# mLSTM attention and two mixture-of-experts layers on one core: full-row tiles for the decay spread and the third logit block, gate work and constants moved into the units

## The chip, the cores and the metric

The kernel runs on one core of one Trainium2 chip. The metric is the time of one execution on the device in microseconds (us), lower is better. Several executions are timed and the median is taken; one more is recorded by the hardware profiler.

## The reference

Three layers follow each other. Attention is a gated linear recurrence over 768 steps for 2 batches and 8 heads of 40 columns; its output, 1536 tokens of 320 columns, goes through a layer that gives each token to one of 8 experts (192 tokens each, best logits first), and then through a dense layer of 4 experts weighted by given probabilities.

```python
for t in range(S):                                   # attention
    m_new = np.maximum(f_gate[:, :, t] + m, i_gate[:, :, t])
    f_stab = np.exp(f_gate[:, :, t] + m - m_new)
    i_stab = np.exp(i_gate[:, :, t] - m_new)
    m = m_new
    C = f_stab * C + i_stab * outer(v_t, k_t)
    n = f_stab * n + i_stab * k_t
    y[:, :, t] = sigmoid(o_t) * (C @ q_t) / np.maximum(np.abs(n @ q_t), 1.0)
logits = x @ w_gate                                  # first expert layer
order = np.argsort(-logits.flatten())                # tokens are given out in this order
out[mask_e] = np.maximum(x[mask_e] @ w1[e], 0) @ w2[e]
p = domain_probs / (domain_probs.sum(-1) + 1e-9)     # second expert layer
out += p[:, e:e + 1] * (np.maximum(x @ w1[e], 0.0) @ w2[e])
```

## The kernel before

All work is issued in the order of the program; each engine takes its own instructions strictly in that order, and semaphores tie the engines together. The change lies wholly in `attention()`, which fills the first 120 us or so; routing, the first expert layer and the second follow.

Attention cuts the 768 steps into 6 chunks of 128 steps. A **unit** is one chunk of one batch with its 8 heads; the 12 units run in the order (0,0), (0,1), (1,0), ... and are numbered n = 0 to 11. For each unit:

- `spread_d` (L244, L246) builds in PSUM (tile `db`, 2 buffers) the sums of the log decay gates over pairs of steps: one matmul with the identity adds a causal mask (`maskb`), and a second one spreads a row of the decay over all 128 partitions. That row is kept as a high and a low part (`dhi`, `dlo`) in `drow`, so this second matmul has 2 rows: `one2` of [2, 128] against `drow` of [2, 512]. The rows get into `drow` by small DMAs (L218), issued by SyncE (SP), one for each chunk and part.
- `exps` (L300, L303) takes the exponential on ScalarE (tile `gg`); `scores` (L287) multiplies keys and queries into `st` (2 buffers); `weigh` (L309) multiplies the two on VectorE into `pm`, which also frees the `st` buffer; `products` (L336, L342, L346) multiplies with the values, with the carried state `C`, and makes the update of the state.
- `epilogue` works on VectorE: `tq` (L371) or a copy (L375), the sum, the normaliser, `xr` (L402), and the update of `C` (L385) in between. It then sends `xr` to DRAM (L404), for which SP also waits for a small load of `dprob` (L401).
- `logit` and `logit2` are the three transposes (L416), the copy to `xt` (L420, L421) and the product with the gate weights `wg` (L433) for earlier units. The 320 columns go in blocks of 128, 128 and 64. The logits are read by VectorE (L435), and the PSUM buffer of a transpose is free again only after that.

`weave` takes matmuls in turn from the generators of a step: in the step of unit n stand the scores of unit n+1, the products of unit n, the spread of unit n+2 and the logits of units n-3 and n-2. The epilogue of unit n follows the step. Matmuls on zeros (`warm`, L254) are put in places where TensorE would wait at the start; `CR['W']` and `CR['W1']` are their numbers there.

`gate(c0, c1)` (L206 to L221) computes the gates of chunks c0 to c1 for all 16 heads on VectorE: two scans and six or seven elementwise instructions, with the DMAs to `drow` between them; `gate_t` transposes the result on TensorE (L233) and copies it to `gtr` (L236). Gates are computed as `gate(0, 1)`, `gate(1, 2)` and, before the loop over the units, `gate(2, NCH)`.

`routing_consts()` (L90 to L123) fills the tables for the routing, 20 instructions on VectorE and the rest on GpSimd, in one block after the epilogue of unit 2. At the top of every second step, `load(c + 2)` and `load_kv(c + 2)` (L154, L161) issue the queries, keys and values of a later chunk on SP, 1320 KB and 648 KB.

## Time and profile before

| | |
|---|---|
| median of 3 executions | 663.55 us (663.23 to 669.81) |
| profiled execution, its own time | 666.88 us |
| span of its trace | 665.2 us |
| granted TensorE clock, mean over the span | 0.975 |
| TensorE matmul busy | 635.1 us (95%) |
| VectorE, ScalarE, GpSimd busy | 281.3, 172.9, 112.8 us |

Times inside the trace count from the start of the span. PE is TensorE, PEld its weight loads, DVE is VectorE, ACT ScalarE, POOL GpSimd, SP SyncE; SPq is SP's sequencer, which issues DMAs. The granted clock is 1 where TensorE runs at 2.4 GHz and 0.5 where it runs at 1.2 GHz.

### The profile page before, as it was taken

Reading aid. Unit: us, or ns where it says so; the run is one execution under the profiler, and the core shown is the slowest. Engines: PE = TensorE matmul, PEld = TensorE weight load, DVE = VectorE, ACT = ScalarE, POOL = GpSimd, SP = SyncE. Lnnn points to the kernel's source line nnn. Section 1 sums busy time; section 2 is a strip of 40 time slices with the busy share of each in tenths; the row PEclk is TensorE's granted clock in tenths of the full one; section 3 lists DMA queues with packets and bytes.
Section 4 is the critical chain, followed back from the end, with each engine's and each line's share of the span. In section 5 each row is a group of like instructions: output and inputs, shape, how many; then the busy total and the mean of one; then the engine's idle time right before and its main releaser. Section 6 shows DMA issues by size and latency. Waiting matters only on the chain.

```text
span 665.2 us, 10604 instructions
## 1 busy us (share of the span) xinstructions
PE 635.1 (95%) x4255; PEld 545.8 (82%) x4265; DVE 281.3 (42%) x1011; ACT 172.9 (26%) x432; POOL 112.8 (17%) x142
## 2 busy tenths in 40 slices
PE   6989999989899999799999999999999999999996
PEld 3778788658588878688898988989889898998986
DVE  4864657774766775531131313313132231322231
ACT  4444331002132323453231112321123211111120
POOL 2321300120122011220331003320023300002022
PEclk7986999899999999999999999999999999999999
DMA  8666421540555233760221001210000000001011
GB/s 218 200 172 161 120 75 31 186 174 3 179 174 179 89 126 140 294 233 0 65 64 48 0 1 33 90 53 1 1 1 0 1 1 0 1 1 41 0 40 39
DMA packets 13503, 53.78 MB, mean 81 GB/s; under 512 B 3639, under 2 KB 5607, under 8 KB 10679
## 3 DMA queue, kind: packets, MB, share of 16 engines
q1 hardware_dynamic: 9695, 27.76, 14.5%
q0 software_dynamic: 3584, 25.26, 10.5%
q8 instruction: 33, 0.54, 0.3%
q10 hardware_dynamic: 176, 0.09, 0.1%
q14 instruction: 15, 0.12, 0.1%
HBM read 49.05 MB, written 3.96 MB: 80 GB/s over the span
## 4 chain that ended last, share of the span: by engine, by line
PE 65%; issue 20%; DVE 10%; POOL 2%; DMA 1%; ACT 1%; POOLq 0%; DVEq 0%; ACTq 0%
PE y L579 5%; PE y L577 5%; PE y L578 5%; PE y L993 5%; PE z L1007 5%; PE z L563 4%; PE z L565 4%; PE z L564 4%; PE st L287 4%; PE z L1087 3%; PE acc L336 3%; PE z L568 2%; PE z L569 2%; POOL out_dram L589 2%; PE z L1000 2%
## 5 line engine op out<-in xcount | busy, mean ns | idle before, releaser
L1227 DVE SCALAR_TENSOR_TENSOR h2l<-z,h2h 128x512 fp32r<-128x512 f32 x96 | 66.4, 692 | 246.1 <-ACT h2h L1226 244.9
L1226 ACT ACTIVATE h2h<-z 128x512 fp32r<-128x512 f32 x96 | 57.3, 597 | 258.7 <-PE z L569 254.4
L579 PE MATMUL y<-wh,h2l 128*128 128x320 f32 x384 | 118.7, 309 | 0.0
L577 PE MATMUL y<-wh,h2h 128*128 128x320 f32 x384 | 118.4, 308 | 0.0
L578 PE MATMUL y<-wl,h2h 128*128 128x320 f32 x384 | 118.1, 308 | 0.0
L563 PE MATMUL z<-X2h,wh 128*128 128x512 f32 x192 | 76.7, 399 | 0.6 <-ACT yt L1027 0.6
L577 PEld LDWEIGHTS y<-wh,h2h 128*128 128x128 f32 x384 | 72.1, 188 | 4.4
L565 PE MATMUL z<-X2h,wl 128*128 128x512 f32 x192 | 75.7, 394 | 0.0
L564 PE MATMUL z<-X2l,wh 128*128 128x512 f32 x192 | 75.3, 392 | 0.0
L578 PEld LDWEIGHTS y<-wl,h2h 128*128 128x128 f32 x384 | 72.1, 188 | 3.8
L579 PEld LDWEIGHTS y<-wh,h2l 128*128 128x128 f32 x384 | 72.0, 188 | 0.0
L552 POOL TENSOR_TENSOR wl<-raw,wh 128x512 fp32r<-128x512 f32 x27 | 34.9, 1292 | 182.6 <-ACT wh L547 182.6
L993 PE MATMUL y<-h,w 128*128 128x192 f32 x256 | 56.0, 337 | 0.2 <-ACT h L1010 0.2
L1007 PE MATMUL z<-xt,w 128*128 128x192 f32 x256 | 54.5, 335 | 0.0
L993 PEld LDWEIGHTS y<-h,w 128*128 128x128 f32 x256 | 41.6, 190 | 2.8 <-issue 1.3
L287 PE MATMUL st<-qk 120*128 120x128 f32 x192 | 43.3, 319 | 0.5 <-issue 0.3
L565 PEld LDWEIGHTS z<-X2h,wl 128*128 128x128 f32 x192 | 36.0, 188 | 9.4
L1007 PEld LDWEIGHTS z<-xt,w 128*128 128x128 f32 x256 | 41.9, 190 | 2.2 <-issue 1.8
L563 PEld LDWEIGHTS z<-X2h,wh 128*128 128x128 f32 x192 | 36.0, 188 | 5.3 <-ACT yt L1027 0.9
L564 PEld LDWEIGHTS z<-X2l,wh 128*128 128x128 f32 x192 | 36.0, 188 | 4.6
L1087 PE MATMUL z<-hot,ones 128*128 128x396 bf16 x199 | 38.3, 330 | 0.4 <-DVE logits L435 0.3
L1010 ACT ACTIVATE h<-z 128x192 f32<-128x192 f32 x64 | 21.0, 330 | 66.8 <-PE z L1007 59.8
(242 smaller groups left out, 923.0 us busy)
## 6 DMA issues: line engine op xcount, KB each, us to landing
raw<-in_m2w_dram SPq DMA_DIRECT2D x20, 512.0 KB, 3.7
qk<-in_qk_dram SPq DMA_DIRECT2D x5, 1320.0 KB, 9.9
kv<-in_kv_dram SPq DMA_DIRECT2D x6, 648.0 KB, 10.5
x_dram<-xr SPq DMA_DIRECT2D x12, 162.0 KB, 2.0
sig<-in_og_dram SPq DMA_DIRECT2D x1, 1280.0 KB, 14.3
raw<-in_m2w_dram SPq DMA_DIRECT2D x4, 256.0 KB, 3.5
qk<-in_qk_dram SPq DMA_DIRECT2D x2, 480.0 KB, 6.4
sig<-in_og_dram SPq DMA_DIRECT2D x1, 640.0 KB, 5.3
```

What stands on the lines that cost most here:

```text
L287: T.matmul(p[:, i], QK[c][:, 6 + h], QK[c][:, 3 * b + (4 * u + i) // 3], start=True, stop=True)
L563: T.matmul(z, hi[:, c], xh[:, k], start=(k == 0), stop=False)
L564: T.matmul(z, hi[:, c], xl[:, k], start=False, stop=False)
L565: T.matmul(z, lo[:, c], xh[:, k], start=False, stop=False)
L577: T.matmul(y[:, :DM], hh[:, ts], hi[:, c], start=(f == 0), stop=False)
L578: T.matmul(y[:, :DM], hh[:, ts], lo[:, d], start=False, stop=False)
L579: T.matmul(y[:, :DM], hl[:, ts], hi[:, c], start=False, stop=(f == NF - 1))
L993: T.matmul(ys[0][:, i * CAP:(i + 1) * CAP], w[:, c:c + P], hs[f], start=(f == 0 and i == 0), stop=(f == NF - 1), skip_group_check=True)
L1007: T.matmul(at(f), w[:, c:c + P], xt[:, k], start=False, stop=(k == 1), skip_group_check=True)
L1087: T.matmul(z[:, :396], ones, hot, start=True, stop=True)
L1226: A.activation(hh, z, AF.Relu)
L1227: V.scalar_tensor_tensor(hl, z, 0.0, hh.bitcast(F32), op0=OP.max, op1=OP.subtract)
```

## The change

- `drow` becomes three tiles of [128, 16 heads, 128], taken in turn by chunk (c % 3), zero but for the two rows of the decay. `one2` becomes [128, 128], zero but for two rows of ones. The spread matmul so has 128 rows. Two of the tiles are cleared by ScalarE copies at the start, the third by a GpSimd memset before the loop.
- The third block of the logits takes columns 192 to 319 in place of 256 to 319; the third block of `wg` has zeros in the rows that stand for columns already counted. Transpose and product have 128 rows and columns, and one ScalarE copy fills `xt` in place of two.
- `gate()` returns a list of steps. Chunks 2 and 3 are put into the epilogue of unit 0 and chunks 4 and 5 into those of units 2 (five steps) and 3 (four steps), each behind the steps of the state update. `gate_t(1, 2)` moves to just before the loop, `gate_t(2, 4)` to the top of step 2, `gate_t(4, NCH)` to the top of step 5.
- `routing_consts()` issues its GpSimd part at once (in a slightly different order) after unit 2 and returns 13 small VectorE pieces, of which three are issued after each epilogue from unit 2 on.
- `CR['W']` goes from 9 to 15 and `CR['W1']` from 3 to 8.

```diff
     def routing_consts():
-        V.tensor_scalar(tri, jp, 0.0, None, op0=OP.is_gt)
...
+        return [lambda: V.tensor_scalar(tri, jp, 0.0, None, op0=OP.is_gt),
+                lambda: V.tensor_scalar(trin, jp, 0.0, -1.0, op0=OP.is_gt, op1=OP.mult),
+                lambda: V.tensor_scalar(triun, jp, 0.0, -1.0, op0=OP.is_lt, op1=OP.mult),
+                lambda: (V.memset(crow, 0.0), V.memset(crow[:1, 1:2], float(CAP)), V.memset(pen, 0.0)),
...
-            drow = big.tile([2, NCH, BH, P], F32, name="drow")
-            one2 = big.tile([2, P], F32R, name="one2")
+            drow = [big.tile([P, BH, P], F32, name=f"drow{i}") for i in range(3)]
+            one2 = big.tile([P, P], F32R, name="one2")
...
+            for i in range(2):
+                A.activation(drow[i].rearrange("p h t -> p (h t)").rearrange("p (i t) -> p i t", t=512).bitcast(F32R),
+                             wup[:, None].to_broadcast([P, 4, 512]), AF.Copy)
             load_o(0, CR['SO'])
             sigm(0, CR['SO'])
...
+                def send(i, d):
+                    for c in range(c0, c1):
+                        nc.sync.dma_start(drow[c % 3][i:i + 1], d[:, c * P:(c + 1) * P].bitcast(F32))
+
+                ops = [lambda: V.tensor_tensor_scan(mm[:, s1], ft[:, s], it[:, s], mm[:, c0 * P:c0 * P + 1],
+                                                    op0=OP.add, op1=OP.max),
+                       lambda: V.tensor_add(dl[:, s], ft[:, s], mm[:, s]),
+                       lambda: V.tensor_sub(dl[:, s], dl[:, s], mm[:, s1])]
                 if c0 == 0:
-                    V.memset(dl[:, 0:1], 0.0)
+                    ops.append(lambda: V.memset(dl[:, 0:1], 0.0))
+                ops += [lambda: V.tensor_tensor_scan(g3[64:64 + BH, s], rst[:, s], dl[:, s], 0.0, op0=OP.mult, op1=OP.add),
+                        lambda: V.tensor_sub(io[:, s], it[:, s], mm[:, s1]),
+                        lambda: (V.tensor_scalar(dhi[:, s], g3[64:64 + BH, s], 0.0, None, op0=OP.add), send(0, dhi)),
+                        lambda: (V.tensor_sub(dlo[:, s], g3[64:64 + BH, s], dhi[:, s].bitcast(F32)), send(1, dlo)),
...
-                    T.matmul(d, one2, drow[:, c, h:h + 4].bitcast(F32R), start=False, stop=True)
+                    T.matmul(d, one2, drow[c % 3][:, h:h + 4].bitcast(F32R), start=False, stop=True)
...
-            V.memset(one2.bitcast(F32), 1.0)
+            V.memset(one2.bitcast(F32), 0.0)
+            V.memset(one2[:2].bitcast(F32), 1.0)
...
-            gate(1, 2)
-            gate_t(1, 2)
+            for f in gate(1, 2):
+                f()
...
                 if (c, b) != units[-1]:
-                    rest += RK
+                    rest += RK + GA.pop((c, b), [])
...
-            XR = {}
+            late_gate = gate(4, NCH)
+            XR, RC, GA = {}, [], {(0, 0): gate(2, 4), (1, 0): late_gate[:5], (1, 1): late_gate[5:]}
...
-                for i in range(3):
-                    m = min(P, DM - i * P)
-                    T.transpose(p[:m, i * P:(i + 1) * P], xr[:, i * P:i * P + m], ident)
+                for i, c0 in enumerate((0, P, DM - P)):
+                    T.transpose(p[:, i * P:(i + 1) * P], xr[:, c0:c0 + P], ident)
...
-                A.activation(xt[:, :2], p3[:, :2], AF.Copy)
-                A.activation(xt[:64, 2], p3[:64, 2], AF.Copy)
+                A.activation(xt, p[:, :384].rearrange("p (i t) -> p i t", t=P), AF.Copy)
...
-                    T.matmul(pl, xt[:m, i], wg[:m, E1 * i:E1 * i + w], start=(i == 0), stop=(i == 2))
+                    T.matmul(pl, xt[:, i], wg[:, E1 * i:E1 * i + w], start=(i == 0), stop=(i == 2))
...
             upto(weigh_v, 1)
-            gate(2, NCH)
+            G.memset(drow[2], 0.0)
             weave([spread_d(*units[1])])
+            gate_t(1, 2)
...
-                if n == CR['Y']:
-                    gate_t(2, NCH)
+                if n == 2:
+                    gate_t(2, 4)
+                if n == 5:
+                    gate_t(4, NCH)
...
                 if n == 2:
-                    routing_consts()
+                    RC.extend(routing_consts())
+                for f in RC[:3]:
+                    f()
+                del RC[:3]
...
-        wg[:len(rows), i * E1:(i + 1) * E1] = rows
+        wg[P - len(rows):, i * E1:(i + 1) * E1] = rows
```

## Rows read from the trace of the kernel before

**Rows 1.** The page's first part: busy time of an engine, its share of the span, number of instructions.
```profile
PE 635.1 (95%) x4255; PEld 545.8 (82%) x4265; DVE 281.3 (42%) x1011; ACT 172.9 (26%) x432; POOL 112.8 (17%) x142
```

**Rows 2.** Busy time of each engine in stretches of 2 us (start and end, length, then the engines), with the granted clock (PEclk), the share of the DMA engines and GB/s at the end.
```profile
14.00:16.00 2.00, 2.00 (x12) 2.00 (x11) 0.54 (x1) 0.52 (x3) 0.00 (x0) 0.50 1.03 218
...
22.00:24.00 2.00, 2.00 (x19) 1.94 (x18) 1.90 (x4) 0.74 (x3) 0.83 (x1) 1.00 0.97 407
...
44.00:46.00 2.00, 0.23 (x2) 0.19 (x2) 1.82 (x17) 0.00 (x0) 0.00 (x0) 0.81 0.74 134
46.00:48.00 2.00, 2.00 (x12) 2.00 (x12) 0.55 (x1) 0.00 (x0) 0.00 (x0) 0.50 0.98 236
...
62.00:64.00 2.00, 2.00 (x20) 2.00 (x18) 0.69 (x1) 0.54 (x2) 0.00 (x0) 0.92 1.02 241
...
116.00:118.00 2.00, 1.85 (x9) 1.16 (x11) 1.90 (x9) 0.00 (x0) 0.27 (x1) 0.73 0.24 83
...
120.00:122.00 2.00, 1.67 (x11) 1.30 (x12) 0.93 (x3) 0.00 (x0) 1.07 (x4) 0.92 0.60 117
```

**Rows 3.** VectorE in order of time: the first instruction of the epilogue of units 1, 2, 3, 4, 5 and 6 (start us, duration us).
```profile
32.77 0.49 DVE L375 COPY tot<-acc 128x328 f32<-128x328 f32 x1
39.15 0.50 DVE L371 TENSOR_TENSOR tq<-acc,gtr 128x328 f32<-128x328 f32 x1 [0.30 <-PE acc L342]
51.53 0.50 DVE L371 TENSOR_TENSOR tq<-acc,gtr 128x328 f32<-128x328 f32 x1 [1.35 <-PE acc L342]
64.11 0.50 DVE L371 TENSOR_TENSOR tq<-acc,gtr 128x328 f32<-128x328 f32 x1 [0.37 <-PE acc L342]
71.88 0.50 DVE L371 TENSOR_TENSOR tq<-acc,gtr 128x328 f32<-128x328 f32 x1 [0.37 <-PE acc L342]
80.14 0.50 DVE L371 TENSOR_TENSOR tq<-acc,gtr 128x328 f32<-128x328 f32 x1 [0.37 <-PE acc L342]
```

**Rows 4.** Engines in order of time around the constants (start us, duration us; in brackets the idle time before and what ended it), and the same logit read of a later unit.
```profile
42.53 0.91 DVE L402 TENSOR_TENSOR xr<-tot,sr 128x320 f32<-128x320 f32 x1
43.36 0.21 DVE L90 TENSOR_SCALAR tri<-jp 128x128 bf16<-128x128 int32 x1
...
45.60 0.16 DVE L435 TENSOR_SCALAR logits<-acc 128x8 f32<-128x8 f32 x1
45.82 0.47 PE L416 MATMUL acc<-ident,xr 128*128 128x128 f32 x1 [1.77 <-DVE logits L435]
...
68.49 0.17 DVE L435 TENSOR_SCALAR logits<-acc 128x8 f32<-128x8 f32 x1 [1.15 <-PE acc L433]
```

**Rows 5.** Engines in order of time at the start.
```profile
6.55 1.27 ACT L169 ACTIVATE sig<-sig 128x1280 f32<-128x1280 f32 x1 [4.00 <-DMA sig<-in_og_dram]
6.57 0.58 SPq L218 DMA_DIRECT2D drow<-dlo  x1
10.73 0.63 PE L244 MATMUL db<-maskb,identb 128*128 128x512 bf16 x1
18.82 0.49 PE L287 MATMUL st<-qk 120*128 120x128 f32 x2
```

**Rows 6.** The gate's instructions over the attention stage, shapes kept apart (number, busy us, mean ns, then idle time before them): 128 and 512 columns.
```profile
L206 DVE TENSOR_TENSOR_SCAN mm<-gt,mm 16x512 f32<-16x512 f32 x1 | 1.3, 1274 | 0.0
L206 DVE TENSOR_TENSOR_SCAN mm<-gt,mm 16x128 f32<-16x128 f32 x2 | 1.2, 619 | 2.1 <-DMA gt<-in_gates_dram 2.1
L213 DVE TENSOR_TENSOR_SCAN g<-rst,dl 16x512 f32<-16x512 f32 x1 | 1.2, 1216 | 0.0
L213 DVE TENSOR_TENSOR_SCAN g<-rst,dl 16x128 f32<-16x128 f32 x2 | 0.8, 416 | 0.1
L208 DVE TENSOR_TENSOR dl<-gt,mm 16x512 f32<-16x512 f32 x1 | 0.7, 678 | 0.0
L208 DVE TENSOR_TENSOR dl<-gt,mm 16x128 f32<-16x128 f32 x2 | 0.6, 279 | 0.1
```

**Rows 7.** The DMAs of a chunk's loads in order of time: issues by SP (SPq), and the GpSimd instruction that waited for the last of them.
```profile
11.84 0.43 SPq L166 DMA_DIRECT2D sig<-in_og_dram  x1
...
29.07 0.59 SPq L154 DMA_DIRECT2D qk<-in_qk_dram  x1
...
30.14 0.43 SPq L401 DMA_DIRECT2D xr<-in_dprob_dram  x1
...
40.30 0.74 POOL L320 TENSOR_TENSOR wv<-kv,gtr 128x328 f32<-128x328 f32 x1 [4.94 <-DMA kv<-in_kv_dram]
40.40 0.33 SPq L404 DMA_DIRECT2D x_dram<-xr  x1
```

**Rows 8.** DMA issues by line of the first 60 us: how often, KB each, us from issue to landing; the second load of `sig`.
```profile
sig<-in_og_dram SPq DMA_DIRECT2D x1, 1280.0 KB, 14.3
```

**Rows 9.** All DMAs into the tile `drow`, us from issue to landing.
```profile
DMA to landing us min/median/max: 1.8/3.0/5.7
```

**Rows 10.** Groups of instructions with shapes kept apart (columns as in rows 6): the spread of 2 rows, a matmul of the second expert layer with the same 512 columns and 128 rows, the smaller copy to `xt`, and `weigh`.
```profile
L563 PE MATMUL z<-X2h,wh 128*128 128x512 f32 x192 | 76.7, 399 | 0.6 <-ACT yt L1027 0.6
...
L309 DVE TENSOR_TENSOR pm<-st,gg 128x512 f32<-128x512 f32 x24 | 16.5, 689 | 22.2 <-PE st L287 21.7 <-ACT gg L303 0.5
...
L246 PE MATMUL db<-drow,one 2*128 2x512 f32 x24 | 13.3, 554 | 1.2 <-issue 0.4
...
L421 ACT ACTIVATE xt<-acc 64x128 f32<-64x128 f32 x12 | 3.1, 260 | 0.0
```

More of the change, by code (lines that the diff above doesn't have):

```diff
@@ L89, in routing_consts @@
     def routing_consts():
[L90 to L99 removed]
+        sp = ct([P, 320], I32, name="sp")
+        dp_ = ct([P, 16], I32, name="dp_")
+        G.iota(sp, pattern=[[1, 320]], base=-64, channel_multiplier=-16)
+        G.iota(dp_, pattern=[[-1, 16]], base=16, channel_multiplier=1)
         G.iota(cand, pattern=[[1, NC]], base=1, channel_multiplier=0, allow_small_or_imprecise_dtypes=True)
         G.iota(cand0, pattern=[[1, LAST + 1]], base=0, channel_multiplier=0, allow_small_or_imprecise_dtypes=True)
[L102 removed]
         G.iota(iota16, pattern=[[1, 16]], base=0, channel_multiplier=0, allow_small_or_imprecise_dtypes=True)
[L104 to L111 removed]
         G.iota(ids, pattern=[[P, NCH], [S, B]], base=0, channel_multiplier=1, allow_small_or_imprecise_dtypes=True)
@@ L116, in routing_consts @@
                         base=-1, channel_multiplier=0)
-        V.memset(pen, 0.0)
-        V.memset(ones16, 1.0)
-        V.memset(need_b, -float(CAP))
-        V.memset(aid, 0.0)
-        V.memset(left, 0.0)
         G.iota(pidx, pattern=[[0, 1]], base=0, channel_multiplier=1, allow_small_or_imprecise_dtypes=True)
         G.iota(prow, pattern=[[0, 1]], base=-P, channel_multiplier=1, allow_small_or_imprecise_dtypes=True)
+        G.memset(hot, 1.0)
+        return [lambda: V.tensor_scalar(tri, jp, 0.0, None, op0=OP.is_gt),
+                lambda: V.tensor_scalar(trin, jp, 0.0, -1.0, op0=OP.is_gt, op1=OP.mult),
+                lambda: V.tensor_scalar(triun, jp, 0.0, -1.0, op0=OP.is_lt, op1=OP.mult),
+                lambda: (V.memset(crow, 0.0), V.memset(crow[:1, 1:2], float(CAP)), V.memset(pen, 0.0)),
+                lambda: V.memset(ones, 1.0),
+                lambda: V.memset(digs, float(NC)),
+                lambda: V.tensor_scalar(unit, jp, 0.0, None, op0=OP.is_equal),
+                lambda: (V.memset(head, 0.0), V.memset(head[:LAST], 1.0)),
+                lambda: V.tensor_scalar(sp, sp, 4, None, op0=OP.arith_shift_right),
+                lambda: V.tensor_scalar(spread, sp, 0.0, None, op0=OP.is_equal),
+                lambda: (V.tensor_scalar(dp_, dp_, 15, None, op0=OP.bitwise_and),
+                         V.tensor_scalar(diag, dp_, 0.0, None, op0=OP.is_equal)),
+                lambda: V.memset(ones16, 1.0),
+                lambda: (V.memset(need_b, -float(CAP)), V.memset(aid, 0.0), V.memset(left, 0.0))]
     logits = keys.tile([P, NT, E1], F32, name="logits")
@@ L214, in gate @@
-                V.tensor_scalar(dhi[:, s], g3[64:64 + BH, s], 0.0, None, op0=OP.add)
-                V.tensor_sub(dlo[:, s], g3[64:64 + BH, s], dhi[:, s].bitcast(F32))
-                for c in range(c0, c1):
-                    for i, d in enumerate((dhi, dlo)):
-                        nc.sync.dma_start(drow[i:i + 1, c], d[:, c * P:(c + 1) * P].bitcast(F32))
-                V.tensor_sub(g3[0:BH, s], io[:, s], g3[64:64 + BH, s])
-                d3 = g3[64:64 + BH, s].rearrange("p (c t) -> p c t", t=P)
@@ L225, in attention @@
+                return ops
             GT = {}
@@ L258, in attention @@
             weave([warm(CR['W'])])
-            gate(0, 1)
+            for f in gate(0, 1):
+                f()
             V.tensor_scalar(ident, jp, 0.0, None, op0=OP.is_equal)
             V.tensor_scalar(identb, jp, 0.0, None, op0=OP.is_equal)
-            V.memset(one2.bitcast(F32), 1.0)
+            V.memset(one2.bitcast(F32), 0.0)
+            V.memset(one2[:2].bitcast(F32), 1.0)
             load_kv(0)
@@ L459, in attention @@
             weave([scores(0, 0)])
-            if CR['W2']:
-                weave([warm(CR['W2'])])
             upto(weigh_v, 1)
-            gate(2, NCH)
+            G.memset(drow[2], 0.0)
             weave([spread_d(*units[1])])
+            gate_t(1, 2)
             for n, (c, b) in enumerate(units):
@@ L486, in attention @@
                 if n == 2:
-                    routing_consts()
+                    RC.extend(routing_consts())
+                for f in RC[:3]:
+                    f()
+                del RC[:3]
             weave([logit2(*units[-3]), logit(*units[-2])])
```

36 lines of the change are left out of this document (6 added, 30 removed).

## The prediction

> **What bounds the kernel now.** The page's first part puts TensorE at 95% of the span and VectorE at 42% [rows 1]. That is an average; the change lies in attention, so I read the stretches of 2 us next, for the granted clock. The clock is full except in three places [rows 2]: the start (0.50 at 14 to 16), a long stretch in the middle and a short one at the end. The shares of the mixed rows give the edges: 0.81 in 44 to 46 means full until 45.2; 0.92 in 62 to 64 means low until 62.3; 0.73 and 0.92 around the short one give 116.9 to 120.3. So the clock is low for 17.1 us and for 3.4 us.
>
> The first instructions of the epilogues then give each unit its price [rows 3]. From unit 4 to 5 it is 7.77 us: an undisturbed unit. From unit 2 to 3 it is 12.38, from 3 to 4 12.58, so the two cost 24.96 in place of 15.54. From 5 to 6 it is 8.26, 0.49 over, in a unit whose epilogue carries rank work. What starts the long low stretch shows where the engines are read side by side [rows 4]: after unit 2's `xr`, VectorE works on constants from 43.36; the logit read L435 stands behind them and comes at 45.60; TensorE idles 1.77 us for it, in the stretch in which the clock falls.
>
> What the low clock costs: unit 4's step is 4.81 over 7.77 and had the low clock from 51.53 to 62.3, 10.8 us. That is 0.45 us for each us of low clock.
>
> **The change, part by part.**
>
> *Constants.* The block is 45.60 - 43.36 = 2.24 us [rows 4]. In 13 pieces, three behind each epilogue, it is about 0.5 us in each of units 2 to 5. Behind it on VectorE stands the next step's L435, and TensorE's transposes wait for that. The slack there is 1.15 us: so long VectorE waits for TensorE before L435 in an undisturbed unit [rows 4]. So 0.5 us alone is hidden, and the stall of 1.77 goes, unless other work takes its place.
>
> *Gates.* It does. No row has 256 columns; between 128 and 512 [rows 6] a third of the way gives 0.84 us for the first scan, 0.68 for the second, 0.41 for an elementwise instruction; the cast L214 I put at 0.28 between those. Nine steps are 0.84 + 0.68 + 6 x 0.41 + 0.28 = 4.3 us; the first five 2.75, the last four 1.5. In unit 2: 2.75 + 0.5 of constants - 1.15 of slack = a stall of 2.1 us in the step of unit 3. In unit 3: 1.5 + 0.5 - 1.15 = 0.85. In unit 5, where rank work already has used the slack up (0.49 over), 0.5 more. With a full clock, units 2 to 4 are then 15.54 + 2.1 + 0.85 = 18.5 in place of 24.96: **-6.5**; unit 6: **+0.5**. A late L435 costs nothing if TensorE itself is late then.
>
> *Start.* Gone before the loop are the nine gate instructions of 512 columns. TensorE's first spread stood at 10.73, because the gates of chunk 1 were in front of it on TensorE's queue, and the loop began at 18.82 [rows 5]. Now the first spread needs `dlo`, issued at 6.57, and 1.8 to 3.0 us to land [rows 9], so about 9.4. The 8.1 us from 10.73 to 18.82 had the low clock; with the warm matmuls now filling the waits I take 5.5, so the loop starts near 15. If the clock isn't held it is 17 to 18; below it doesn't matter which. The added matmuls (6 and 5) sit in waits for VectorE. ScalarE's two fills of `drow` are bounded by `sig`: 1.27 us for 1280 columns [rows 5], so some 1.9 for 2048 and 3.8 for both, inside the 4.00 us in which ScalarE waits for the DMA.
>
> *The rows of chunks 2 and 3.* Here I see the main new wait. Before, SP issued them before the loop, in front of the loads of chunk 2. Now `load(2)` and `load_kv(2)`, 1320 and 648 KB, are issued at the top of the loop and the rows behind them, out of the epilogue of unit 0. What stands behind those loads waits: `dprob`, a small load, was issued at 30.14 behind them, and L404, which waits for it, came at 40.40, right after the last of the loads had let GpSimd go at 40.30 [rows 7]. Before, the rows themselves landed within 1.8 to 5.7 us [rows 9].
> When do they land now? `sig` is in front of all: issued at 11.84 [rows 7] with 14.3 us to landing [rows 8], 26.1. Then the pair of loads. Upper bound: 11.2 us (29.07 to 40.3), out of an empty queue [rows 7]; less the shortest landing of a small transfer, 1.8, that is 9.4. Lower bound: 1.97 MB at the best rate of a stretch, 407 GB/s [rows 2], 4.8. It is the same pair, so I stay near the upper end: 8.5, and the rows land at 34.6 (30.9 to 37.3).
> And when does TensorE want them? The two units from 18.82 to 32.77 took 13.95 [rows 3, 5], so unit 0's epilogue starts near 15 + 7 = 22. It holds VectorE for about 3.4 of its own (unit 2's, from 39.15 to 43.36, was 4.2 with more in it [rows 3, 4]) and 4.3 of gates, until 29.7; then comes `weigh`, 0.69 [rows 10], which frees the buffer for the scores of step 2. Step 2 starts at 30.4 and wants the row of chunk 2 in its first round, at about 31.3. So TensorE stands still for some 3 us there, everything on its queue behind the spread. From the first round to the epilogue's start I take the old unit, 39.15 - 32.77 = 6.4 [rows 3], less 0.9: 34.6 + 5.5 = 40.1, against 39.15: **+0.95**. The whole gain of the start is gone by then, whatever it was, and no later wait of the start (an early low clock, one table load more on ScalarE) counts either.
>
> *The clock after that wait.* TensorE has idled about 1 us at 29.7 and 3 us behind it; a stall of 1.77 was enough before [rows 4], so it falls. No row tells how long it stays down with the new rows. The bounds are the two stretches above, 3.4 and 17.1 us; I take 6, nearer to the short one, since what follows is dense work with full rows: 6 x 0.45 = **+2.7**.
>
> *Full rows.* The matmuls have as many columns as before. With 128 rows, 512 columns and the same type the second layer's take 399 ns against 554 for the spread over both clocks [rows 10]: no dearer. One copy to `xt` less saves ScalarE at most 260 ns a unit [rows 10], beside other work but at the tail: **-0.2**.
> On the clock the rows themselves speak for them: from 14 to 16 TensorE is busy 2.00 of 2.00 and yet at half clock [rows 2], and spreads of 2 rows were among what it had done just before. The Trainium skill, "TensorE: Matmul & The Clock Gate", section "What's actually happening", lets the clock follow how busy the engine has been of late, with no word of rows; by it the fuller rows change nothing and the low stretch would be like the old one. The trace does not agree with busy time as the only measure, but it doesn't show either that rows are the missing one.
>
> **Sum.** +0.95 + 2.7 - 6.5 + 0.5 - 0.2 = -2.55 us. On the profiled execution, 666.88, that is 664.3; the median of the runs shown lies 3.3 below that execution, 663.55, and 663.55 - 2.55 = **661.0**. With L us of low clock in the middle it is 658.3 + 0.45 L.
>
> **The rivals.**
> 1. *The rows are in time.* If the loads run near 407 GB/s they land at 30.9, before step 2 wants them at 31.3. Then unit 2's epilogue starts at 30.4 + 6.4 = 36.8, 2.35 early, and no low stretch follows: -2.35 - 6.5 + 0.5 - 0.2 = -8.55: **655.0**. For it: 407 GB/s was reached; against it: this very pair took 11.2.
> 2. *The clock stays low* (the other side). Place: from the wait in step 2 on. The stalls of 2.1 and 0.85 in units 3 and 4 hit just when the clock could come back, and the first is as long as the one that brought it down before. Price: 0.45 for each us. With the old stretch, 17.1, the time is 658.3 + 7.7 = **666.0**, slower by 0.4%; it turns at L = 11.7, and beyond L = 26 it is slower by 1%. For it: TensorE was 2.00 of 2.00 busy from 46 to 48 and the clock did not rise [rows 2]; against it: a late TensorE hides VectorE's stalls. The rule of the skill above would end here.
> 3. *It doesn't do what it says at the start*: the warm matmuls don't hold the clock. Then the loop starts at 17 to 18 and step 2 near 33, and the rows still come last: 661 as well, a case of the forecast.
>
> **How the numbers follow.** The forecast (658.3 to 663.5, with the wait and 3 to 11 us of low clock) has 0.44, rival 3 in it; rival 1, with shorter waits between, 0.30; rival 2 0.26. About 1% of the time, 6.6 us, is what a measurement of this kernel can tell from no change. Faster by more than that needs a time under 656.9, nearly all of rival 1: 0.28. Slower by more is rival 2 with L over 26 us, or with the rows as late as 37.3 (+2.7): 0.10. Within 1%: 0.62. The range goes 2 us below rival 1, since the gates' stalls may be smaller, and to L = 21 above: 653 to 668.
>
> **What would show it.** In the changed kernel's trace: the spread of chunk 2 waiting for a DMA into `drow`, TensorE idle 2 to 5 us near 31; the stage's rows with a clock of 0.5 behind it; L416 waiting for L435 by some 2 us in step 3 if the clock is full there, and by about 1 us in steps 4 and 6; the first spread near 9.4. The prediction is wrong where that DMA isn't what comes last, where the clock isn't lost behind it, or where VectorE takes the gates in less than the slack.

## The result and the profile after

The changed kernel takes 672.4 us (median of four executions, 668.6 to 674.7) against 663.5: a ratio of 1.0147, interval 1.0102 to 1.0191, slower by about 9 us. The forecast was 661.0 with a range to 668. Its profiled execution, 668.6 us with a span of 666.9, is the fastest of the four.

Of the profile after, first the page's first part, as in [rows 1]. TensorE is busy 10 us less than before (624.9 against 635.1) in a longer span:

```profile
PE 624.9 (94%) x4276; PEld 544.4 (82%) x4276; DVE 283.9 (43%) x1021; ACT 176.7 (27%) x426; POOL 116.3 (17%) x143
```

The first instruction of the epilogues of units 0 to 6 on VectorE (start us, duration), as in [rows 3], shows where:

```profile
21.05 0.49 DVE L378 COPY tot<-acc 128x328 f32<-128x328 f32 x1
30.36 0.48 DVE L378 COPY tot<-acc 128x328 f32<-128x328 f32 x1
44.83 0.50 DVE L374 TENSOR_TENSOR tq<-acc,gtr 128x328 f32<-128x328 f32 x1 [0.30 <-PE acc L345]
57.55 0.50 DVE L374 TENSOR_TENSOR tq<-acc,gtr 128x328 f32<-128x328 f32 x1 [1.35 <-PE acc L345]
66.99 0.50 DVE L374 TENSOR_TENSOR tq<-acc,gtr 128x328 f32<-128x328 f32 x1 [0.38 <-PE acc L345]
74.63 0.50 DVE L374 TENSOR_TENSOR tq<-acc,gtr 128x328 f32<-128x328 f32 x1 [0.37 <-PE acc L345]
86.71 0.50 DVE L374 TENSOR_TENSOR tq<-acc,gtr 128x328 f32<-128x328 f32 x1 [0.40 <-PE acc L345]
```

Unit 1 is 2.4 us earlier than before, unit 2 is 5.7 later (44.83 against 39.15), unit 4 only 2.9 later (66.99 against 64.11), unit 6 again 6.6 later (86.71 against 80.14). So two steps lose: that of unit 2, 14.47 us in place of 6.38, and that of unit 6, 12.08 in place of 8.26. What TensorE waits for longest names them. PE in order of time, idle time and its end in brackets (the first line is the first spread of all, which waits for nothing):

```profile
9.13 0.38 PE L245 MATMUL db<-maskb,identb 128*128 128x512 bf16 x1
14.75 0.46 PE L290 MATMUL st<-qk 120*128 120x128 f32 x2 [1.21 <-DMA qk<-in_qk_dram]
38.28 0.77 PE L247 MATMUL db<-drow,one 128*128 128x512 f32 x1 [7.52 <-DMA drow<-dlo]
51.80 0.47 PE L419 MATMUL acc<-ident,xr 128*128 128x128 f32 x1 [3.11 <-DVE logits L435]
81.97 0.41 PE L419 MATMUL acc<-ident,xr 128*128 128x128 f32 x1 [3.48 <-DVE logits L435]
```

The clock falls at each of the three. Stretches of 2 us, columns as in [rows 2]:

```profile
14.00:16.00 2.00, 1.05 (x6) 0.73 (x6) 0.00 (x0) 1.09 (x7) 1.17 (x1) 1.00 1.10 233
30.00:32.00 2.00, 0.76 (x5) 0.44 (x5) 1.97 (x9) 0.00 (x0) 0.13 (x1) 0.73 0.88 183
40.00:42.00 2.00, 2.00 (x13) 1.71 (x12) 0.00 (x0) 1.30 (x7) 0.00 (x0) 0.71 0.23 58
50.00:52.00 2.00, 0.20 (x1) 0.20 (x2) 1.92 (x9) 0.00 (x0) 0.00 (x0) 0.85 0.51 185
60.00:62.00 2.00, 2.00 (x11) 1.81 (x10) 1.89 (x5) 1.93 (x5) 1.60 (x2) 0.59 0.02 6
82.00:84.00 2.00, 2.00 (x11) 2.00 (x12) 0.71 (x2) 0.00 (x0) 0.00 (x0) 0.53 0.88 225
118.00:120.00 2.00, 1.36 (x14) 1.17 (x13) 1.76 (x6) 0.49 (x1) 0.00 (x0) 1.00 0.29 88
```

The mixed rows give the edges as in the prediction: low from 30.9 to 41.1, from 51.4 to 61.6, and 3.4 us from 82.1. The start is full now (14 to 16), but that gain is in the 2.4 us of unit 1 already. What gives back some of the 6.6 us behind unit 6 are shorter steps (from unit 6 to unit 11 31.2 us in place of 33.5) and the end, where the kernel before had a short fall of the clock [rows 2]. The profiled span is only 1.7 us longer than that of the kernel before.

The issues on SP's queue in order of time show why the rows come late (start us, duration; x2 are two issues, for chunks 2 and 3):

```profile
15.31 0.35 SPq L161 DMA_DIRECT2D sig<-in_og_dram  x1
15.71 0.43 SPq L149 DMA_DIRECT2D qk<-in_qk_dram  x1
16.18 0.38 SPq L156 DMA_DIRECT2D kv<-in_kv_dram  x1
27.45 1.15 SPq L208 DMA_DIRECT2D drow<-dhi  x2
28.69 1.17 SPq L208 DMA_DIRECT2D drow<-dlo  x2
```

The rows, 8 KB a transfer, are issued 11 to 12 us behind three large loads, and land some 10 us after their issue (38.28 less 28.69); before, no row transfer took over 5.7 [rows 9]. By the times to landing `sig` lands at 30.5, `qk` at 36.1, `kv` at 37.7 and the rows right behind it. Bytes alone are not the whole wait: from 36 to 38 the DMA engines are busy for a share of only 0.04 (17 GB/s), and what holds the last 2 us isn't shown.

**How executions differ.** Each execution comes with its span and mean granted clock. With levels of one half and one, 2 x (1 - clock) x span is the time at low clock, and span x clock is what is left of the span when half of that time is taken off. The four executions of the changed kernel:

| span, us | clock | span x clock | low clock, us |
|---|---|---|---|
| 666.9 | 0.981 | 654.2 | 25.3 |
| 669.5 | 0.974 | 652.1 | 34.8 |
| 671.9 | 0.970 | 651.7 | 40.3 |
| 673.0 | 0.972 | 654.2 | 37.7 |

The profiled execution has the least low clock of the four, and less than the profiled one of the kernel before (25 against 33 us). The 9 us between the medians are the 1.7 of the two profiles, 3.8 by which the profiled execution lies under its kernel's median, and 3.3 by which the one before lies above its own. So the profiles account for 1.7 us; the 35 to 40 us of low clock in the other three executions stand in no trace.

By the way it is worked out, two executions with the same product lie 0.5 us apart for each us of low clock, so the table can't tell what low clock costs. The spread of many executions can: over 20 of the kernel before, run beside e9 to e12, low clock goes from 5.2 to 76.3 us and the span from 656.2 to 680.9, 0.35 each; over the four of e4 from 17.1 to 64.1 and from 659.1 to 682.3, 0.49. The prediction took 0.45 from one step. The Trainium skill, "TensorE: Matmul & The Clock Gate", section "Terms", prices low clock by the share of pulses left out, which is 0.5 here; e4 agrees, and the kernel before stays under it. Nor is the product constant: it goes from 654 to 643 over those 20 as low clock grows. So the two columns tell lost work from lost clock only roughly, and best between runs with about as much low clock.

### The profile page after: what moved, and what is told of

Read it like the earlier page. It is cut to its first block, busy times and chain, and to the rows that moved or that the text cites. A ratio compares the mean times of both kernels' runs of the same rounds, so it can differ in the third digit from the quotient of the medians.

```text
span 666.9 us, 10653 instructions
## 1 busy us (share of the span) xinstructions
PE 624.9 (94%) x4276; PEld 544.4 (82%) x4276; DVE 283.9 (43%) x1021; ACT 176.7 (27%) x426; POOL 116.3 (17%) x143
## 4 chain that ended last, share of the span: by engine, by line
PE 45%; issue 19%; DVE 4%; DMA 2%; POOL 2%; ACT 1%; POOLq 0%
PE y L583 5%; PE y L581 5%; PE y L582 5%; PE z L567 4%; PE z L569 4%; PE z L568 4%; PE z L1011 4%; PE y L997 4%; DMA xg<-x_dram,tok 2%; PE z L572 2%; PE z L573 2%; POOL out_dram L593 2%; PE z L1004 2%; PE y L1021 1%; PE pd L967 1%
## 5 line engine op out<-in xcount | busy, mean ns | idle before, releaser
L290 PE MATMUL st<-qk 120*128 120x128 f32 x192 | 41.2, 305 | 2.4 <-DMA qk<-in_qk_dram 1.2
## 6 DMA issues: line engine op xcount, KB each, us to landing
sig<-in_og_dram SPq DMA_DIRECT2D x1, 1280.0 KB, 15.2
```

The source lines that it names most:

```text
L290: T.matmul(p[:, i], QK[c][:, 6 + h], QK[c][:, 3 * b + (4 * u + i) // 3], start=True, stop=True)
```

## The experiments

Theory: the loss is rows of chunk 2 queued behind loads, then VectorE work (gates, constants) standing in front of the logits, each with a fall of the clock. Rivals: the full rows or the longer warming cost time; the constants alone do it. The last two columns are medians. The kernel before had 646 and 32 in them beside e1 to e4, 652 and 33 beside e5 to e8, 646 and 31 beside e9 to e12, and 648 and 36 beside e13 and e14; runs of different groups are compared by their ratios, and by times only roughly.

| run | us | before beside it | ratio, interval | span x clock | low clock, us |
|---|---|---|---|---|---|
| changed kernel | 672.4 | 663.5 | 1.015 (1.010 to 1.019) | 653 | 36 |
| e1 | 665.5 | 663.0 | not given | 649 | 29 |
| e2 | 656.3 | 663.0 | 0.985 (0.976 to 0.995) | 646 | 18 |
| e3 | 682.3 | 663.0 | 1.026 (1.015 to 1.036) | 651 | 63 |
| e4 | 672.3 | 663.0 | not given | 650 | 41 |
| e5 | 664.6 | 668.8 | 0.992 (0.988 to 0.996) | 644 | 39 |
| e6 | 657.6 | 668.8 | 0.983 (0.979 to 0.987) | 647 | 17 |
| e7 | 660.8 | 668.8 | 0.988 (0.984 to 0.993) | 651 | 17 |
| e8 | 654.1 | 668.8 | 0.978 (0.974 to 0.983) | 645 | 16 |
| e9 | 672.0 | 664.8 | 1.012 (1.008 to 1.016) | 651 | 37 |
| e10 | 651.7 | 664.8 | 0.979 (0.974 to 0.985) | 645 | 11 |
| e11 | 654.4 | 664.8 | 0.983 (0.978 to 0.989) | 645 | 18 |
| e12 | 666.6 | 664.8 | 1.001 (0.997 to 1.005) | 650 | 33 |
| e13 | 660.7 | 667.3 | 0.988 (0.978 to 0.997) | 650 | 19 |
| e14 | 676.2 | 667.3 | 1.014 (1.008 to 1.021) | 655 | 38 |

### e1: the loads of chunk 2 behind the rows

```diff
-                    if c + 2 < NCH:
+                    if 2 < c + 2 < NCH:
...
                 epilogue(c, b)
+                if n == 0:
+                    load(2)
+                    load_kv(2)
```


> The changed kernel with one edit: the queries, keys and values of chunk 2 are issued behind the epilogue of unit 0, so the rows of chunks 2 and 3 stand in front of them on SyncE's queue. Theory one (the rows wait behind those loads): TensorE's 7.5 us without work in front of the spread of chunk 2, seen in the changed kernel from 30.8 to 38.3, shrinks to under 2 us, and unit 2's epilogue starts near 39 in place of 44.8; what is given back is a wait of up to 2 us for the loads themselves in step 3. Time 4 to 6 us under the changed kernel's. Theory two (VectorE's gates are the wait in step 2, the DMA only comes last by a little): the start of unit 2's epilogue moves by under 1.5 us and the time by under 2 us.

Four executions from 660.4 to 675.3. The wait for `drow` is gone and unit 2's epilogue starts at 40.0 in place of 44.8. The next in line is VectorE, which now has the late gates while TensorE is on time:

```profile
43.97 0.77 PE L290 MATMUL st<-qk 120*128 120x128 f32 x2 [3.62 <-DVE dl L213]
```

So the late rows are part of the loss, but not all of it. The medians are 7 us apart, which executions that differ by 15 us price only roughly; e12 gives the better price.

### e2: all gates of chunks 2 to 5 before the loop

```diff
-            drow = [big.tile([P, BH, P], F32, name=f"drow{i}") for i in range(3)]
+            drow = [big.tile([P, BH, P], F32, name=f"drow{i}") for i in range(NCH)]
...
-            G.memset(drow[2], 0.0)
+            for c in range(2, NCH):
+                G.memset(drow[c], 0.0)
+            for f in gate(2, NCH):
+                f()
...
-                if n == 2:
-                    gate_t(2, 4)
-                if n == 5:
-                    gate_t(4, NCH)
+                if n == 1:
+                    gate_t(2, NCH)
```


> The changed kernel with the gates of chunks 2 to 5 computed in one block before the loop, as in the kernel before; six row tiles in place of three, so that no row waits for an earlier chunk's spread; the transposes of these gates stand at the top of step 1. Full rows, the third logit block, the constants in pieces and the warm matmuls stay. Theory one (gates in the epilogues and the late rows made the loss): the waits in steps 2 and 3 (7.5 and 3.1 us) go, the one in step 6 (3.5 us) stays, steps without a wait stay at 6.85 us, and the time is 650 to 657, under both kernels. Theory two (full rows, or the constants, lose the time): 668 or more, with waits still in steps 3 and 6.

Faster than both kernels. Against the kernel before beside it, the low clock is what is less (18 us against 32), and span x clock is equal (646). No wait for rows is left; the longest that stay are 2.5 us for `qk` and 1.9 for the logits in the step with the ranking. It keeps full rows, pieces and warming, so none of these is what made the change slower.

### e3: the changed kernel with spreads of two rows

```diff
-T.matmul(d, one2, drow[c % 3][:, h:h + 4].bitcast(F32R), start=False, stop=True)
+T.matmul(d, one2[:2], drow[c % 3][:2, h:h + 4].bitcast(F32R), start=False, stop=True)
```


> The changed kernel with one edit: the spread matmul takes two rows of the same tiles instead of all 128. All data and their order stay. Theory one (the full rows shorten the step): undisturbed steps 7 to 9 go from 6.85 us back to about 7.8, and the time rises by up to 6 us, less what the waits for VectorE shrink by, since a longer step covers them. Theory two (the shorter step comes from the third logit block or the single copy to xt): steps 7 to 9 stay at 6.85 us. On the clock: if full rows bring it back sooner, the low stretch behind the wait in step 2, 10.2 us with them, becomes longer here; if they do nothing, it stays about as long.

Slower than the changed kernel, by 10 us in the medians and 7 by the ratios. An undisturbed step takes 7.6 us in place of 6.85, and the low clock is 63 us in place of 36: no execution has under 50, none of the changed kernel over 41. In the profile the low stretch behind the wait for the rows goes from 30.6 to 58.7, 28 us in place of 10.2. Most of the lost time is thus clock, and span x clock is not longer (651 against 653). Where the extra 0.75 us of a step lies is seen in one spread. This run's weight loads (PEld) and matmuls in order of time, idle time in brackets:

```profile
105.19 0.18 PEld L247 LDWEIGHTS db<-drow,one 2*128 2x128 f32 x1 [0.32 <-issue]
105.19 0.50 PE L247 MATMUL db<-drow,one 2*128 2x512 f32 x1
105.61 0.30 PEld L433 LDWEIGHTS acc<-wg,xt 128*128 128x128 f32 x2 [0.25 <-issue]
```

The same place of a step in the changed kernel:

```profile
95.51 0.38 PE L245 MATMUL db<-maskb,identb 128*128 128x512 bf16 x1
95.52 0.19 PEld L247 LDWEIGHTS db<-drow,one 128*128 128x128 f32 x1
95.54 0.58 PE L247 MATMUL db<-drow,one 128*128 128x512 f32 x1
95.73 0.42 PEld L433 LDWEIGHTS acc<-wg,xt 128*128 128x128 f32 x2
```

The load of two rows starts 0.32 us late, and the load behind it 0.25 late; with full rows both run beside the matmul in front. From 60 to 115 us all 12 of the two-row loads have such idle time before them, and none of the 11 of the changed kernel. The loads themselves are equally long (0.18 and 0.19). Two spreads a step have about 1.1 us of such idle, of which 0.75 shows in the step.

### e4: the kernel before with the constants in pieces

```diff
-                    routing_consts()
+                    RC.extend(routing_consts())
+                for f in RC[:3]:
+                    f()
+                del RC[:3]
```

`routing_consts()` itself is that of the changed kernel.

> The kernel before with one part of the change: the constants in 13 pieces, three behind each epilogue from unit 2 on. Theory one (the block of constants starts the long low clock): TensorE's wait of 1.77 us in step 3 goes, the clock stays at its upper level from 18 to about 113, and the time falls by 7 to 10 us, to 654 to 657. Theory two (another wait takes its place): the pieces run longer beside GpSimd's work than in the block, as they did in the changed kernel's unit 5 (0.85, 0.70 and 0.66 us in place of 0.33, 0.17 and 0.17), step 6 gets a wait over 1.5 us, the clock falls there, and the gain is under 3 us.

The stall of 1.77 [rows 4] and the long low stretch behind it are gone from its profile, with the steps to units 3, 4 and 5 at 7.8 us each. The step to unit 6, behind an epilogue with constants and ranking, takes 10.50 with a wait of 0.9 us for the logits at its start (theory two had over 1.5), and the clock falls elsewhere (27.2 to 34.0, 71.6 to 75.0, 112.5 to 115.9). Four executions lie between 660.8 and 684.0, so the time is inconclusive.

### e5: the kernel before with full rows alone

```diff
-            drow = big.tile([2, NCH, BH, P], F32, name="drow")
-            one2 = big.tile([2, P], F32R, name="one2")
+            drow = [big.tile([P, BH, P], F32, name=f"drow{i}") for i in range(NCH)]
+            one2 = big.tile([P, P], F32R, name="one2")
...
```

The row tiles of chunks 0 and 1 are filled by ScalarE, as in the change, those of chunks 2 to 5 zeroed by GpSimd.

> The kernel before with full-row spread matmuls alone (128-row row tiles and ones, six tiles, zeroed before the loop), nothing else of the change. Theory A (a spread matmul of two rows leaves its weight load exposed, a full one hides it): undisturbed steps go from 7.77 to about 6.9 us; eight to ten steps give 7 to 8 us, so about 656. Theory B (the shorter steps of the changed kernel come from elsewhere, the gates or the constants): steps stay 7.77 and the time stays within 1% of the kernel before, 660 to 667; the longer zeroing on GpSimd may cost 1 to 2 us at the start.

0.8% faster, ten executions. Undisturbed steps take 6.99 us in place of 7.77 (82.96 to 89.96 below), the gain that the prediction put at nothing. So theory A's step is there, and span x clock is 9 us less than beside it (644 against 652), but its time of about 656 is not: the low clock is not less than before (39 us against 33), and full rows alone do not bring it back.

```profile
75.97 0.50 DVE L375 TENSOR_TENSOR tq<-acc,gtr 128x328 f32<-128x328 f32 x1 [0.37 <-PE acc L346]
82.96 0.50 DVE L375 TENSOR_TENSOR tq<-acc,gtr 128x328 f32<-128x328 f32 x1 [0.38 <-PE acc L346]
89.96 0.50 DVE L375 TENSOR_TENSOR tq<-acc,gtr 128x328 f32<-128x328 f32 x1 [0.37 <-PE acc L346]
```

### e6: e2 with the constants as one block

```diff
-                for f in RC[:3]:
+                for f in RC:
                     f()
-                del RC[:3]
+                RC.clear()
```


> The run with the gates of chunks 2 to 5 before the loop, but the constants as one block behind the third epilogue instead of three an epilogue. Theory A (the pieces are what removes the wait of TensorE for the logits of step 3): one wait of 1.8 us or more at that step and the clock falls there, 2 to 6 us slower than that run, about 659 to 662. Theory B (pieces only move the wait to other steps): within 1% of it, 653 to 660, with no wait behind step 6.

The wait of 2.9 us for the logits is back in its profile, and a low stretch from 43.7 to 57.4, but the ratio is that of e2 within the intervals. Splitting the constants moves the wait and saves nothing that these executions can tell.

### e7: e2 with the loads of chunk 2 first again

```diff
+            load(2)
+            load_kv(2)
             load_o(CR['SO'], NCH)
...
-                    if c + 2 < NCH:
+                    if 2 < c + 2 < NCH:
...
-                for f in RC[:3]:
+                k = (0, 0, 3, 3, 3, 0, 2, 2)[n] if n < 8 else 0
+                for f in RC[:k]:
```


> The run with the gates of chunks 2 to 5 before the loop, with two more changes: the loads of chunk 2 are issued ahead of the large load of the output gate, and no constant is computed in the epilogue that already holds the ranking. Theory A (its waits of 2.5 us for the third chunk and 1.9 us for the logits, and the clock that falls behind them, are what is left of the loss): both waits gone, about 650 to 654. Theory B (those waits are replaced by the next in line, the output gate landing late or VectorE's own total): within 1% of 656.

A miss that settles the row question: meant to take away e2's wait for `qk`, it put the loads in front of the rows again, and the wait of the changed kernel returned.

```profile
15.45 0.32 SPq L149 DMA_DIRECT2D qk<-in_qk_dram  x1
15.82 0.40 SPq L156 DMA_DIRECT2D kv<-in_kv_dram  x1
16.26 0.43 SPq L161 DMA_DIRECT2D sig<-in_og_dram  x1
20.50 2.41 SPq L208 DMA_DIRECT2D drow<-dhi  x4
...
37.27 0.77 PE L247 MATMUL db<-drow,one 128*128 128x512 f32 x1 [7.28 <-DMA drow<-dlo]
```

Here the gates were early and the rows issued 5 to 7 us earlier than in the changed kernel (20.50 and 23.50 against 27.45 and 28.69); they still came last. What stands in front of them counts more than when they are issued. The price is 4 to 6 us of span x clock at as much low clock (651 against 647 in e6 and 645 in e8, the nearest kernels beside it).

### e8 and e9: fewer warming matmuls, in e2 and in the changed kernel

```diff
-'W1': 8,
+'W1': 3,
...
-'W': 15,
+'W': 9,
```


> The run with the gates of chunks 2 to 5 before the loop, with the 9 and 3 warming matmuls of the kernel before instead of 15 and 8. Theory A (the longer warming holds the clock up through the start): a low clock of about 10 us from about 7.7 us on returns and costs 3 to 5 us, about 659 to 661. Theory B (the warming delays as much work as the clock gives back): within 1% of 656, with the first score up to 2 us earlier.

> The changed kernel with the 9 and 3 warming matmuls of the kernel before instead of 15 and 8; nothing else. Theory A (the twelve extra matmuls of 0.21 us delay the start by up to 2.5 us and the clock they hold gives back no more than that): 2 to 3 us less than the changed kernel, ratio to the kernel before about 1.010; the wait for the rows of the low part at the third unit stays about 7 us. Theory B (the clock they hold is worth more): slower than the changed kernel by 2 us or more, ratio 1.018 or above.

Neither shows a difference beyond its interval. In e8 the clock is low at 7.9 to 11.4 and 25.0 to 28.4 instead, and its ratio is the lowest, level with e10's. In e9 (11 matmuls fewer, not twelve) the wait for the rows is 4.03 us and ends at 35.28, 3 us earlier than in the changed kernel: `sig`, issued at the same time, lands 11.1 us after its issue in place of 15.2, and why isn't shown. Unit 2's epilogue starts at 42.85, and the stalls for the logits are as long as the changed kernel's (the longest 3.5). The longer warming buys nothing here: in e9 too the clock is full up to 30 us, and unit 0's epilogue starts at 21.02, in the changed kernel at 21.05.

### e10: e8 with the third logit block of 64 rows

```diff
-                for i, c0 in enumerate((0, P, DM - P)):
-                    T.transpose(p[:, i * P:(i + 1) * P], xr[:, c0:c0 + P], ident)
+                for i in range(3):
+                    m = min(P, DM - i * P)
+                    T.transpose(p[:m, i * P:(i + 1) * P], xr[:, i * P:i * P + m], ident)
...
-                A.activation(xt, p[:, :384].rearrange("p (i t) -> p i t", t=P), AF.Copy)
+                A.activation(xt[:, :2], p3[:, :2], AF.Copy)
+                A.activation(xt[:64, 2], p3[:64, 2], AF.Copy)
...
```


> The run with gates before the loop and 9 and 3 warming matmuls, with the third logit block of 64 rows and two copies on ScalarE as in the kernel before. Theory A (the logit block is worth next to nothing, 0.2 us at the tail): within 2 us of that run, ratio 0.976 to 0.982. Theory B (full rows matter there as in the spread): undisturbed steps longer by 0.2 us or more and 2 to 4 us slower, ratio 0.982 to 0.985.

Steps are 7.0 us with 64 rows against 6.82, but the ratio is that of e8. The full logit block is worth at most 0.2 us a step.

### e11: e8 without constants in the ranking's epilogue

```diff
-                for f in RC[:3]:
+                k = (0, 0, 3, 3, 3, 0, 2, 2)[n] if n < 8 else 0
+                for f in RC[:k]:
```


> The run with gates before the loop and 9 and 3 warming matmuls, with no constant computed in the epilogue that holds the ranking. Theory A (the wait of 1.9 us for the logits behind that epilogue is the constants'): no wait over 1.3 us for the logits and the time 1 to 2 us less, ratio 0.975 to 0.978. Theory B (the ranking alone makes it): unchanged, with a wait of 1.5 us or more at that step.

The wait for the logits falls to 1.3 us; waits for `qk` take its place (4.8 us in three), and the time does not change.

### e12 and e13: only the first gates before the loop, and the constants out of the others' way

```diff
-{(0, 0): gate(2, 4), (1, 0): late_gate[:5], (1, 1): late_gate[5:]}
+{(1, 0): late_gate[:5], (1, 1): late_gate[5:]}
...
             weave([spread_d(*units[1])])
+            for f in gate(2, 4):
+                f()
```

e13 has besides:

```diff
-                for f in RC[:3]:
+                k = 3 if n in (4, 6, 7, 9) else 1 if n == 10 else 0
+                for f in RC[:k]:
```


> The changed kernel with the gates of chunks 2 and 3 moved from the first epilogue to before the loop, so that their rows are queued ahead of the loads of chunk 2; the gates of chunks 4 and 5 stay between the epilogues of units 2 and 3, and the three rotating tiles stay. Theory A (the late rows are the loss; gates between epilogues cost nothing): the wait for the rows is gone and the time comes near the run with all gates before the loop, ratio 0.98 to 0.99. Theory B (the gates of chunks 4 and 5 between epilogues cost VectorE time that TensorE waits for as well): a wait of 2.5 us or more for the logits of step 3 remains, the clock falls there, ratio 0.995 to 1.005.

> The changed kernel with the gates of chunks 2 and 3 before the loop (as in the run on that), and the constants only from the fifth epilogue on, so that the epilogues of units 2 and 3 hold the gates of chunks 4 and 5 and no constant. Theory A (the gates' own operations make the wait for the logits of step 3): a wait of 2.5 us or more stays there, ratio 0.99 to 1.00. Theory B (the constants beside them make it): that wait falls under 1.5 us, the clock holds through steps 3 and 4, and the ratio is 0.985 or less.

e12's wait for the rows ends at 30.95 in place of 38.28 and it gains 1.4% on the changed kernel's ratio, up to the kernel before and no further: the waits for the logits in steps 3 and 6 stand (3.42 and 3.48 us), with low clock from 44.1 to 47.5 and 74.8 to 85.1, and it is low from 54.4 to 64.6 as well, behind one of 1.46 in step 4. In e13, with the constants moved away, the one in the ranking's step falls to 1.31 and that of step 3 to 2.70:

```profile
45.22 0.33 PE L419 MATMUL acc<-ident,xr 128*128 128x128 f32 x1 [2.70 <-DVE logits L435]
53.27 0.33 PE L419 MATMUL acc<-ident,xr 128*128 128x128 f32 x1 [1.06 <-DVE logits L435]
69.21 0.33 PE L419 MATMUL acc<-ident,xr 128*128 128x128 f32 x1 [1.31 <-DVE logits L435]
```

So the gates make most of the wait of step 3 and the constants most of that of step 6. Neither side had it whole: the gates' wait stays as theory A of e13 said, and the time falls under its range. Span x clock is that of e12 (650); what it gains is clock, 19 us low in place of 33, though it still waits 2.20 us in front of the spread at 30.49.

### e14: the rows of chunks 2 and 3 from ScalarE's queue

```diff
-nc.sync.dma_start(drow[c % 3][i:i + 1], d[:, c * P:(c + 1) * P].bitcast(F32))
+(nc.scalar if c0 == 2 else nc.sync).dma_start(drow[c % 3][i:i + 1], d[:, c * P:(c + 1) * P].bitcast(F32))
```


> The changed kernel with the row transfers of chunks 2 and 3 issued from ScalarE's queue instead of SP's, at the same place of the program. Theory A (their place behind the loads in one queue makes them late): they land within 3 us of their issue, by about 32 us, the third unit waits no more than 1 us for them, and the ratio falls to 0.995 to 1.003. Theory B (the transfer engines are busy with the loads whatever the queue): they land after 36 us, the wait of 5 us or more stays, ratio 1.010 to 1.018.

No faster. The issue stands at the same time, and the first row lands 8.2 us behind it, at 35.6; ScalarE and TensorE then wait until 36 to 37.5:

```profile
27.39 1.24 ACTq L208 DMA_DIRECT2D drow<-dhi  x2
28.73 7.42 ACTq L208 DMA_DIRECT2D drow<-dlo  x2
36.19 0.17 ACT L303 ACTIVATE dec<-db 120x4 f32<-120x4 f32 x1 [17.66 <-DMA drow<-dlo]
...
37.45 0.59 PE L245 MATMUL db<-maskb,identb 128*128 128x512 bf16 x1 [6.81 <-ACT dec L303]
```

Another queue did not pass the loads: from 28 to 34 us the DMA engines are busy for a share of 0.88 to 0.91. The last issue was held for most of 7.42 us as well, and ScalarE with it; what held it isn't shown. TensorE's wait here is for ScalarE, so the run's time is not that of the late rows alone.

## Why the prediction was wrong

**Right: the start.** The first spread at 9.13 (9.4 said), the loop's first score at 14.75 (15), unit 0's epilogue at 21.05 (22), the clock held; and all of it was taken by the rows of chunk 2, as said. For the clock that was luck, as far as the reason goes: e9, with the old number of warm matmuls, holds it as well.

**Mis-sized: when the rows land.** The wait was named and placed (near 31, behind the loads), but it was 7.5 us, not 3. TensorE wanted the row at 30.8 (31.3 said); the landing was put at 34.6, at most 37.3, and was about 38.2. One link was taken over from before: `sig`, in front of the pair, issued at 11.84 [rows 7]. It now went out at 15.31 (SP waited 3.2 us in front of it, which the profile puts down to the landing of `wg`) and landed at 30.5 in place of 26.1; the pair then took 7.2 us, not more than the 8.5 said. With step 2 at low clock behind it, the term of +0.95 at unit 2's epilogue was +5.7. e1, e7 and e12 show this cause, and e14 that another queue did not remove it.

**Wrong: one fall of the clock.** The sum had a single stretch of 6 us behind the rows. There were three, 10.2, 10.2 and 3.4: each long stall for the logits brought its own. The price of a microsecond, 0.45, was of the right size (0.35 and 0.49 over executions). Rival 2 had the direction and the place of the first fall, but not the cause of the loss: in the profile the low clock in all is shorter than before (25 us against 33), and what was lost there is waits.

**Mis-sized: VectorE's stalls.** Step 3 stalled 3.11 us, not 2.1, and step 6 3.48, where the whole step was put at +0.5 over the old one and was +3.8. The stall of 0.85 said for step 4 was 0.60. Epilogue of unit 2, VectorE:

```profile
46.74 1.31 DVE L210 TENSOR_TENSOR_SCAN mm<-gt,mm 16x256 f32<-16x256 f32 x1
48.20 0.66 DVE L212 TENSOR_TENSOR dl<-gt,mm 16x256 f32<-16x256 f32 x1
...
51.18 0.22 DVE L105 TENSOR_SCALAR tri<-jp 128x128 bf16<-128x128 int32 x1
...
51.59 0.16 DVE L435 TENSOR_SCALAR logits<-acc 128x8 f32<-128x8 f32 x1
```

The interpolated 0.84 for the first scan was 1.31 and the 0.41 for an elementwise step 0.66; in unit 0 the scan took 0.74, and the steps behind these two in unit 2 took the 0.41 and 0.68 said. In unit 5, three small constants beside GpSimd's work took 0.85, 0.70 and 0.66 us, after a wait for GpSimd's ranking step that the sum had not looked for:

```profile
78.67 0.35 DVE L517 TENSOR_REDUCE rank<-rk 128x24 f32<-128x192 f32 x1 [1.16 <-POOL rk L516]
...
79.59 0.85 DVE L114 TENSOR_SCALAR spread<-sp 128x320 f16<-128x320 int32 x1
80.23 0.81 POOL L359 TENSOR_TENSOR tmpc<-C,dec 120x328 f32<-120x328 f32 x1
80.37 0.70 DVE L115 TENSOR_SCALAR dp__520<-dp__520 128x16 int32<-128x16 int32 x1
81.00 0.73 POOL L323 TENSOR_TENSOR wv<-kv,gtr 128x328 f32<-128x328 f32 x1
81.10 0.66 DVE L116 TENSOR_SCALAR diag<-dp__520 128x16 f32<-128x16 int32 x1
```

In e2 the same three take 0.31, 0.16 and 0.17, with no GpSimd instruction beside them. The slack of 1.15 also shrank, to 0.44 and 0.33, since a step is 0.9 shorter. So the -6.5 of units 2 to 4 was -2.8 (22.16 against 24.96 us). All terms up to unit 6's epilogue made -2.35 in the sum; the trace has +6.6 there.

**Missed: the full rows.** Put at "no dearer" from the lengths of single matmuls, they shorten each undisturbed step by 0.8 us (e3, e5), because the weight loads no longer stand alone. The view that tells it was there in the trace of the kernel before: the idle time of PEld in front of the two-row loads, which the prediction doesn't use (first 120 us; number, busy us, mean ns, then idle time before them):

```profile
L246 PEld LDWEIGHTS db<-drow,one 2*128 2x128 f32 x24 | 4.9, 202 | 7.9 <-issue 7.9
```

The gain stands in e2, e8 and e10 too (undisturbed steps of 6.8 to 7.0 us); how much of their time is its and how much the clock's (11 to 18 us low against 31 to 33 beside them) the runs don't separate. In the changed kernel 2.3 us of it show behind unit 6, and the waits take more.

**Open.** Why the clock stays low for 63 us with two-row spreads in the changed kernel and only 31 to 36 in the kernel before, why executions of one kernel differ by 20 us and more of low clock, and so where the median's loss beyond the profile's 1.7 us lies. Settled by the runs: moving all gates back before the loop and keeping the rest is 1.5% faster than before (e2), and with the old warming 2.2% (e8, 654.1 us; e10 alike), which e2's interval holds too.

## What to carry to other kernels

A small transfer on which the next step hangs is issued ahead of the large loads, and its landing is worked out from all the loads in front of it at their new issue times; another queue did not save it here. VectorE work that is slipped in between steps costs nothing only as far as the slack in front of the next read goes, and that slack shrinks when the same change makes the step shorter. A gap that is closed shows up as time only if the next gap behind it is closed too, and each gap that stays can cost the clock once more, as three did here.

## What the hardware showed

A weight load of two rows was not started beside the matmul in front of it, one of 128 rows was (0.32 and 0 us of idle before equally long loads). The Trainium skill, "TensorE: Matmul & The Clock Gate", section "Architectural detail: the array is 16× 32×32, not 1× 128×128", lets TensorE pull weight loads ahead of matmuls in flight, with no word of rows there; the trace agrees for full rows and not for these.

Small VectorE instructions took some three to four times as long beside GpSimd's (L115: 0.70 against 0.16 us in e2), and two of the three above end 0.03 us behind the GpSimd instruction beside them (at 81.07 and 81.76, after 81.04 and 81.73). The Trainium skill, "SBUF — State Buffer", section "Terms", has the two engines take turns at a shared pair of ports, the loser blocked for a whole instruction; the rows agree with that, though no run here took the GpSimd work away by itself.
